# Attention's key blocks merged by predicated copies, PSUM banks redistributed and GpSimd jobs moved, in a fused attention and mixture-of-experts kernel

## The chip, the cores and the metric

The kernel runs on one core of a Trainium2 chip. The metric is the device time of one execution in microseconds, lower is better. The engines of a core run their own queues in order: TensorE (PE; PEld is its weight load), VectorE (DVE), ScalarE (ACT), GpSimd (POOL) and SyncE (SP), which here issues all transfers.

## The reference, cut to what matters

```python
# attention: q, k, v of (2, 8, 576, 64); window 128; ALiBi slopes per head
scores = (q @ k.T) / 8 + slope[h] * -abs(rel)      # rel = row - column
scores = where((rel >= 0) & (rel < 128), scores, -1e9)
attn = exp(scores - max); attn = attn / (attn.sum(-1) + 1e-9)
x = (attn @ v) as (1152, 512)
# first block: 4 experts with 1024 hidden columns each, all tokens through all of them
p = probs / (probs.sum(-1) + 1e-9)
x = sum over e of p[:, e] * (relu(x @ w1[e]) @ w2[e])
# second block: 2048 hidden columns
h = x @ w_in;  out = (h * cos(h)) @ w_out
```

All inputs and the output are fp32; w_in and w_out come in as double precision and are converted by the kernel.

## The kernel before, in words

**Attention.** The 576 rows of each of the two batch entries are cut into five units: unit 0 of 64 rows, units 1 to 4 of 128. A step is one unit and one half of the heads (g = 0 or 1, four heads each), 20 steps in all; unit numbers below are within a batch entry. The keys of a row lie in its own block and in the block ahead of it, so a unit from 1 on has scores of up to 256 columns, of which each row needs 128: where an own key would lie behind the row, the key at the same place of the block ahead is in the window. `attention` (from L464) emits at step k, in this order: `att_scores(k)`, `att_sums(k-1)`, `fill(k, 0)`, `att_transpose(k-3)`, `att_normalise(k-1)`, `fill(k, 1)`, `att_pv(k-4)`, `fill(k, 2)`. `att_scores` makes four score products into two PSUM tiles, then per head one VectorE pass (L362: adds bias and mask, keeps the minimum of the negated scores) and one ScalarE exponential with its sum (L367). `att_normalise` (L383) divides on GpSimd, `att_transpose` (L405) transposes each head's one or two blocks on TensorE and copies them out with VectorE (L415) and ScalarE (L417), `att_pv` (L433) multiplies with the values of both blocks. When both halves of a unit are done, its results leave PSUM: rounded into a high and a low part (`split_x`, L333), or through `transform` (from L273), a generator of nine parts (0 to 8) that builds seven combinations of the x tiles for a Strassen-like product, each as a high part on ScalarE (L278) and a low part, a subtraction (L130) on VectorE or GpSimd. `transformed` first issues what is left of the transform before, then part 0; `move(n)` issues n more parts. `fill` slips other work in: the weight jobs at steps 4 to 19, the first-layer products of group 0 that need plain x (`plain`) at steps 12 to 19 in halves, and the second-layer products `layer2(0, 0)`, `layer2(0, 1)`, `layer2(0, 2)` at steps 21, 22 and 23.

**The groups.** The two blocks are cut into 12 groups of 512 hidden columns: 0 to 7 are the experts, 8 to 11 the second block. Group 7 is called `turn` (its results are flipped by TensorE transposes, f1 to f8, and enter the second block through `transformed`). Every matrix is held as a high and a low part and each product is made of three passes (L537 for the combinations in `product`, L565 in `plain`, L631 in `layer2`). `pair` makes the combinations of two hidden tiles in seven products, in the order A11 B11, S2 T2, S1 T1, S3 T3, A12 B21, S4 B22, A22 T4: a step of `steps` (from L731) each, with ScalarE's copy p1 (L586), VectorE's additions u1 and c22 (L580) and `finish` between them. In groups 8 to 11 `finish` runs `cosine`, a chain of stages on ScalarE, VectorE and GpSimd (its last stage makes the low part of h or hpair, L517 and L130); `advance` issues one stage of every open chain. `layer2(g, t)` reads h for t under 3 and hpair above.

**What sets the order.** All of it is written out by hand, and each engine works through its queue in that order. `steps(g)` yields per TensorE step how many chain stages, weight jobs (`next(jobs)`) and conversion parts (`next(cv)`) are issued between its matmuls and its end; `run` (L783) issues matmuls, then `move(2)`, the stages, the jobs, the conversion parts, then the step's end. A weight job (L155, L172, L185, L130) rounds one 128x512 piece of a weight on ScalarE and subtracts on GpSimd, or makes two of the weight sums on GpSimd; some of them issue the next load on SP's queue. At the end of a group `run` issues what is left of the transforms:

```python
            while moved:
                move(24)
```

**PSUM.** Each bank takes one tile. `ps1` has two banks during the whole kernel; attention has three for scores, two for transposes, one for its results; after attention these six become `mm`. `bank()` (L674) numbers the product tiles: 4 are taken by `plain` and 3 by `layer2` during attention, and the first product of group 0 is number 8.

```python
    def bank():
        count[0] += 1
        return ps1 if mm is None or count[0] % 4 == 0 else mm
```

## Time and profile before

| what | value |
|---|---|
| median of 3 runs (lowest to highest) | 669.71 us (668.44 to 672.1) |
| the profiled execution | 668.45 us |
| its span | 666.7 us |
| busy: PE, PEld | 645.6 us (97%), 568.7 us (85%) |
| busy: DVE, ACT, POOL | 432.8, 335.9, 367.6 us |
| mean granted clock of TensorE | 0.995 |
| HBM | 90 GB/s over the span |

The span runs from the first to the last instruction; about 1.8 us of the execution's own time lie around it. Busy times say how long an engine had an instruction in work; matmuls are pipelined and their ends are modelled, so a busy TensorE is not TensorE at its peak, and gaps between its instructions are the surer sign.

### The profile page before, as it was taken

The page shows a single profiled execution, that of the slowest core. Times are in us where ns is not written, and L with a number is a line of the kernel's source. Part 1 is how long each engine was busy: PE and PEld are TensorE (multiplying, and loading weights), DVE is VectorE, ACT ScalarE, POOL GpSimd, SP SyncE. Part 2 cuts the span into 40 slices and gives each one's busy share as a digit, 9 for nine tenths or more (in the row PEclk, how much of TensorE's full clock was granted, in tenths as well). Part 3 has the DMA queues.
Part 4 walks back from the last instruction along what each step waited for, and adds up shares of the span by engine and source line. Part 5 has one row for each costly group of instructions (what it writes and reads, how often), then busy time and mean ns, then how long its engine had stood idle before and what let it go on. Part 6 is the DMA issues. An engine that isn't in the chain of part 4 may idle for free.

```text
span 666.7 us, 9755 instructions
## 1 busy us (share of the span) xinstructions
PE 645.6 (97%) x3516; PEld 568.7 (85%) x3516; DVE 432.8 (65%) x842; ACT 335.9 (50%) x768; POOL 367.6 (55%) x346
## 2 busy tenths in 40 slices
PE   8989899999999999999999999999799999999997
PEld 5677698998998998988988988988788988988976
DVE  7676776878668578589578562647663563563562
ACT  6878644453344354354343341346684674584560
POOL 3977729356265175183282381465468558558530
PEclk8999999999999999999999999999899999999999
DMA  9162114435417335245236130030101101202002
GB/s 262 41 204 83 32 33 138 130 112 200 128 35 225 106 101 185 79 139 193 80 131 200 32 121 7 32 96 0 33 0 64 65 0 63 65 0 64 17 31 94
DMA packets 39727, 60.40 MB, mean 91 GB/s; under 512 B 5632, under 2 KB 22016, under 8 KB 39680
## 3 DMA queue, kind: packets, MB, share of 16 engines
q1 hardware_dynamic: 39680, 59.80, 28.2%
q8 instruction: 27, 0.44, 0.3%
q14 instruction: 20, 0.16, 0.1%
HBM read 49.04 MB, written 10.75 MB: 90 GB/s over the span
## 4 chain that ended last, share of the span: by engine, by line
PE 78%; DVE 7%; ACT 7%; POOL 4%; issue 2%; DMA 1%; SPq 0%; ACTq 0%; DVEq 0%; POOLq 0%
PE o_ps L631 39%; PE o_ps L537 21%; PE o_ps L565 13%; PE s_ps L350 2%; DVE u L509 2%; ACT r L507 2%; ACT u L506 2%; PE x_ps L433 1%; POOL p L383 1%; POOL w1t L130 1%; PE t_ps L405 1%; POOL hpair L130 1%; DVE o_ps L580 1%; DVE xs L130 1%; DVE u L515 1%
## 5 line engine op out<-in xcount | busy, mean ns | idle before, releaser
L631 PE MATMUL o_ps<-w2t,hpair 128*128 128x512 f32 x864 | 207.3, 392 | 4.3 <-POOL hpair L130 4.1
L631 PEld LDWEIGHTS o_ps<-w2t,hpair 128*128 128x128 f32 x864 | 160.7, 188 | 38.3 <-POOL hpair L130 5.8
L537 PE MATMUL o_ps<-xs,w1t 128*128 128x384 f32 x1008 | 182.5, 338 | 3.9 <-DVE c L580 1.8
L537 PEld LDWEIGHTS o_ps<-xs,w1t 128*128 128x128 f32 x1008 | 177.1, 189 | 7.6 <-DVE c L580 3.1
L130 POOL TENSOR_TENSOR w2t<-raw,w2t 128x512 fp32r<-128x512 f32 x48 | 66.2, 1394 | 82.1 <-ACT w2t L185 82.1
L130 POOL TENSOR_TENSOR w1t<-raw,w1t 128x512 fp32r<-128x512 f32 x48 | 65.0, 1364 | 83.2 <-ACT w1t L155 83.0
L565 PE MATMUL o_ps<-xq,w1t 128*128 128x384 f32 x576 | 110.3, 338 | 0.0
L565 PEld LDWEIGHTS o_ps<-xq,w1t 128*128 128x128 f32 x576 | 101.6, 188 | 3.3
L631 PE MATMUL o_ps<-w2t,h 128*128 128x512 f32 x432 | 103.3, 392 | 0.0
L631 PEld LDWEIGHTS o_ps<-w2t,h 128*128 128x128 f32 x432 | 80.7, 188 | 16.1 <-issue 0.2
L130 POOL TENSOR_TENSOR w1t<-sm,w1t 128x512 fp32r<-128x512 f32 x48 | 64.6, 1356 | 41.9 <-ACT w1t L155 35.1
L509 DVE SCALAR_TENSOR_TENSOR u<-r,u 128x384 f32<-128x384 f32 x48 | 34.6, 726 | 51.7 <-ACT r L507 51.7
L130 POOL TENSOR_TENSOR hpair<-u,hpair 128x384 fp32r<-128x384 f32 x32 | 33.6, 1066 | 42.3 <-ACT hpair L517 42.3
L245 ACT ACTIVATE cr<-cr 128x512 f32<-128x512 f32 x32 | 21.6, 675 | 43.4 <-DVE cv L239 43.4
L367 ACT ACTIVATE p<-p,nmax 128x256 f32<-128x256 f32 (+2 forms) x80 | 36.2, 454 | 13.0 <-DVE nmax L362 12.8
L646 DVE SCALAR_TENSOR_TENSOR accpair<-o_ps,pr,accpair 128x512 f32<-128x512 f32 x42 | 31.3, 745 | 17.3 <-PE o_ps L631 17.3
L233 ACT ACTIVATE cr<-cr 128x512 int32<-128x512 uint32 x32 | 21.6, 675 | 40.7 <-DMA cr<-w_in 25.3
L524 ACT ACTIVATE hpair<-o_ps 128x384 fp32r<-128x384 f32 x48 | 23.4, 488 | 36.6 <-DVE o_ps L580 35.9
L155 ACT ACTIVATE w1t<-sm 128x512 fp32r<-128x512 f32 x48 | 30.0, 627 | 20.3 <-POOL sm L130 20.3
L525 DVE SCALAR_TENSOR_TENSOR hpair<-o_ps,hpair 128x384 fp32r<-128x384 f32 x48 | 26.6, 555 | 20.3 <-ACT hpair L524 20.3
L383 POOL TENSOR_TENSOR p<-p,rec 128x512 f32<-128x512 f32 (+5 forms) x30 | 32.6, 1102 | 9.5 <-DVE rec L377 5.6
L239 DVE SCALAR_TENSOR_TENSOR cv<-cr,cv 128x512 int32<-128x512 int32 x32 | 35.1, 1097 | 1.1
(100 smaller groups left out, 821.3 us busy)
## 6 DMA issues: line engine op xcount, KB each, us to landing
raw<-w SPq DMA_DIRECT2D x32, 512.0 KB, 3.7
cr<-w_in SPq DMA_DIRECT2D x16, 512.0 KB, 4.6
cr<-w_out SPq DMA_DIRECT2D x16, 512.0 KB, 4.5
wi<-cv SPq DMA_DIRECT2D x16, 256.0 KB, 3.6
wo<-cv SPq DMA_DIRECT2D x16, 256.0 KB, 2.3
raw<-wi SPq DMA_DIRECT2D x8, 512.0 KB, 3.5
raw<-wo SPq DMA_DIRECT2D x8, 512.0 KB, 3.5
qt<-qT SPq DMA_DIRECT2D x8, 256.0 KB, 4.9
```

The lines of the kernel that those rows point to most:

```text
L130: eng.tensor_tensor(out=out, in0=a, in1=b, op=ALU.subtract)
L155: nc.scalar.activation(out=hi[:, s], in_=src[:, s], func=AF.Copy)
L239: nc.vector.scalar_tensor_tensor(out=a, in0=hw, scalar=-0x40000000, in1=o, op0=ALU.bitwise_and, op1=ALU.bitwise_or,)
L367: nc.scalar.activation(out=p[:n, k, :wid], in_=p[:n, k, :wid], func=AF.Exp, scale=-1.0, bias=nmax[:n, k : k + 1], accum_out=den[:n, k, 0:1],)
L383: nc.gpsimd.tensor_tensor(out=p[:n, s, :wid], in0=p[:n, s, :wid], in1=rec[:n, s].unsqueeze(2).to_broadcast([n, s.stop - s.start, wid]), op ...
L509: nc.vector.scalar_tensor_tensor(out=u, in0=r, scalar=MAGIC, in1=u, op0=ALU.subtract, op1=ALU.subtract)
L524: nc.scalar.activation(out=hi, in_=src, func=AF.Relu)
L525: nc.vector.scalar_tensor_tensor(out=lo, in0=src, scalar=0.0, in1=hi.bitcast(F32), op0=ALU.max, op1=ALU.subtract)
L537: nc.tensor.matmul(ps, w(a, k, m), xs[:, bb, b, m], start=(start and m == 0 and (a, bb) == PASSES[0]), stop=(stop and m == 1 and (a, bb) = ...
L565: nc.tensor.matmul(ps, w(a, 2 * (q % 2) + d // 2, d % 2), xq[:, bb, d], start=(d == 0 and (a, bb) == PASSES[0]), stop=(d == ND - 1 and (a, ...
L631: nc.tensor.matmul(ps, h0[:, a, f, t * 128 : (t + 1) * 128] if t < NQ else hpair[:, a, f, (t - NQ) * 128 : (t - NQ + 1) * 128], w_t[2, g, ...
L646: nc.vector.scalar_tensor_tensor(out=o, in0=ps, scalar=s, in1=o, op0=ALU.mult, op1=ALU.add)
```

## The change

The scores of the block ahead are copied over those of the unit's own keys, where those lie behind the row: a mask `later` (nonzero there) steers two predicated copies on VectorE, within PSUM, and one block of 128 columns is left. Bias, exponential, normalising and transposing are done on it alone. With merged weights p, the product with the values is p times the values of the block ahead plus (p where the key is the unit's own, by the mask `own`) times the difference of the two blocks' values; the difference is made on GpSimd in `values`. Unit 1, whose block ahead has 64 rows, gets a tile `va` with those rows below 64 rows of zeros, loaded once more.

PSUM: `ps1` has one bank in place of two, scores four, transposes one, results two, and after attention `mm` has seven; `bank` takes ps1 for every eighth tile. Order: the weight jobs of groups 8 to 10 leave layer2(g, 1), layer2(g, 2) and P0 and go to layer2(g, 3), P1 and layer2(g, 4); the rest of a transform is not issued at the end of a group any more but carried on, one part behind each step of a pair. The diff, cut:

```diff
-    ps1 = pool("ps1", bufs=2, space=PSUM)
+    ps1 = pool("ps1", bufs=1, space=PSUM)
...
-    ptp = ap("ptp", bufs=4)
+    ptp = ap("ptp", bufs=2)
+    vdp = ap("vdp", bufs=3)
     stp = ap("stp", bufs=6)
-    ps_s = ap("ps_s", bufs=3, space=PSUM)
-    ps_t = ap("ps_t", bufs=2, space=PSUM)
-    ps_x = ap("ps_x", bufs=1, space=PSUM)
+    ps_s = ap("ps_s", bufs=4, space=PSUM)
+    ps_t = ap("ps_t", bufs=1, space=PSUM)
+    ps_x = ap("ps_x", bufs=2, space=PSUM)
...
+        for e in range(2):
+            for h in range(H):
+                slope = 2.0 ** (-8.0 * (h + 1) / H)
+                if e == 0:
+                    nc.vector.scalar_tensor_tensor(
+                        out=bm[:, e, h], in0=rel, scalar=-8.0 * slope, in1=edge,
+                        op0=ALU.mult, op1=ALU.add,
+                    )
+                else:
+                    nc.gpsimd.tensor_scalar(
+                        out=bm[:, e, h], in0=rel, scalar1=-8.0 * slope, scalar2=None, op0=ALU.mult
+                    )
+            if e == 0:
+                make_identity(nc, ident)
+        nc.gpsimd.memset(va[:64], 0.0)
+        nc.gpsimd.memset(own, 1.0)
...
+        if i == 1:
+            nc.sync.dma_start(out=va[64:], in_=v[b, :64, :])
+    def values(b, i):
+        ahead = va if i == 1 else v_t[b, i - 1]
+        vd = vdp.tile([128, DM], F32, name="vd", tag="vd")
+        nc.gpsimd.tensor_tensor(out=vd, in0=v_t[b, i], in1=ahead, op=ALU.subtract)
+        v_d[b, i] = ahead, vd
...
+        c0 = 128 - (s0 - k0)
...
                 nc.tensor.matmul(
-                    ps[hh][:n, m, :wid], q_t[u][r, 2 * g + m, :n],
+                    ps[hh][:n, m, c0 : 128 + n], q_t[u][r, 2 * g + m, :n],
                     k_t[b][r, 2 * g + m, k0 : s0 + n], start=True, stop=True,
                 )
-        p = ppool.tile([128, 4, 256], F32, name="p", tag="p")
+        p = ppool.tile([128, 4, 128], F32, name="p", tag="p")
...
+        if i:
+            for hh in range(2):
+                nc.vector.copy_predicated(
+                    ps[hh][:n, :, 128 + c0 :], later.bitcast(U32)[:n, :, c0:], ps[hh][:n, :, c0:128]
+                )
         for m in range(2):
             for hh in range(2):
                 k = 2 * m + hh
                 h = 4 * g + k
                 nc.vector.tensor_tensor_reduce(
-                    out=p[:n, k, :wid], in0=ps[hh][:n, m, :wid], in1=bm[:n, h, c0 : c0 + wid],
+                    out=p[:n, k, :n], in0=ps[hh][:n, m, 128 : 128 + n], in1=bm[:n, int(i > 1), h, :n],
                     scale=-0.125, scalar=3.0e38, op0=ALU.add, op1=ALU.min,
...
-        for s in (slice(0, 4),) if u[0] == 0 else (slice(0, 2), slice(2, 4)):
-            nc.gpsimd.tensor_tensor(
-                out=p[:n, s, :wid], in0=p[:n, s, :wid],
-                in1=rec[:n, s].unsqueeze(2).to_broadcast([n, s.stop - s.start, wid]), op=ALU.mult,
-            )
+        nc.gpsimd.tensor_tensor(
+            out=p[:n, :, :n], in0=p[:n, :, :n],
+            in1=rec[:n].unsqueeze(2).to_broadcast([n, 4, n]), op=ALU.mult,
+        )
         state[u, g] = p
...
+        if g == 0 and u[1]:
+            values(*u)
...
-        blocks = list(key_blocks(u[1]))
-        pT = []
-        for m in range(2):
-            tp = ps_t.tile([128, 2, 2, 128], F32, name="t_ps", tag="t_ps")
-            pt = ptp.tile([128, 2, 2, 128], F32, name="pt", tag="pt")
-            for bi, (j, o, ln) in enumerate(blocks):
-                for hh in range(2):
-                    nc.tensor.transpose(
-                        tp[:ln, bi, hh, :n], p[:n, 2 * m + hh, o : o + ln], ident[:n, :n]
-                    )
...
-            for a, bb in sl:
-                if m == 0:
-                    nc.vector.tensor_copy(pt[a, bb, :, :n], tp[a, bb, :, :n])
-                else:
-                    nc.scalar.activation(out=pt[a, bb, :, :n], in_=tp[a, bb, :, :n], func=AF.Copy)
-            pT.append(pt)
-        state[u, g] = pT
+        tp = ps_t.tile([128, 4, 128], F32, name="t_ps", tag="t_ps")
+        for k in range(4):
+            nc.tensor.transpose(tp[:n, k, :n], p[:n, k, :n], ident[:n, :n])
+        pt = ptp.tile([128, 4, 128], F32, name="pt", tag="pt")
+        nc.scalar.activation(out=pt[:n, :, :n], in_=tp[:n, :, :n], func=AF.Copy)
+        po = None
+        if u[1]:
+            po = ptp.tile([128, 4, 128], F32, name="po", tag="po")
+            nc.vector.tensor_tensor(
+                out=po, in0=tp, in1=own.unsqueeze(1).to_broadcast([128, 4, 128]), op=ALU.mult
+            )
+        state[u, g] = pt, po
 
...
-        pT = state.pop((u, g))
-        blocks = list(key_blocks(i))
...
         for m in range(2):
-            for bi, (j, o, ln) in enumerate(blocks):
-                for hh in range(2):
-                    h = 4 * g + 2 * m + hh
-                    nc.tensor.matmul(
-                        xt[64 * hh : 64 * hh + 64, 2 * g + m, :n],
-                        v_t[b, j][:ln, 64 * h : 64 * h + 64],
-                        pT[m][:ln, bi, hh, :n],
-                        start=(bi == 0), stop=(bi == len(blocks) - 1),
-                    )
+            for hh in range(2):
+                k = 2 * m + hh
+                h = 4 * g + k
+                hs = slice(64 * h, 64 * h + 64)
+                o = xt[64 * hh : 64 * hh + 64, 2 * g + m, :n]
+                if i == 0:
+                    nc.tensor.matmul(o, v_t[u][:n, hs], pt[:n, k, :n], start=True, stop=True)
+                    continue
+                ahead, more = v_d[u]
+                nc.tensor.matmul(o, ahead[:, hs], pt[:, k], start=True, stop=False)
+                nc.tensor.matmul(o, more[:, hs], po[:, k], start=False, stop=True)
...
-        return ps1 if mm is None or count[0] % 4 == 0 else mm
+        return ps1 if mm is None or count[0] % 8 == 0 else mm
...
-    mm = pool("mm", bufs=6, space=PSUM)
+    mm = pool("mm", bufs=7, space=PSUM)
...
-            yield layer2(g, 1), 2, 2 if turn else int(not last), 2
-            yield layer2(g, 2), 2, 2 if turn else int(not last), 2
+            yield layer2(g, 1), 2, 2 if turn else int(early), 2
+            yield layer2(g, 2), 2, 2 if turn else int(early), 2
...
-        njobs = 0 if last else 4 if turn else 6 if early else 10
+        njobs = [1] * 10
         if g == 0:
-            njobs += 2
+            njobs = [2, 2, 1, 1, 1, 1]
+        elif turn:
+            njobs = [1] * 4
+        elif early:
+            njobs = [1] * 6
+        elif not last:
+            njobs = [0, 1, 2, 2, 1, 2, 1, 1, 1, 1]
         for k, o in enumerate(order):
-            more = min(njobs, 2 if g == 0 and k < 2 else 1)
+            more = njobs.pop(0) if njobs and not last and str(o)[0] != "f" else 0
...
         for g in groups:
             for step, stages, njobs, ncv in steps(g):
                 next(step)
-                move(2)
+                move(2 if ncv or stages != 1 else 1)
                 for _ in range(stages):
                     advance()
                 for _ in range(njobs):
@@ -792,9 +821,6 @@
                 for _ in range(ncv):
                     next(cv, None)
                 next(step, None)
-            while moved:
-                move(24)
-
```

## Rows read from the trace of the kernel before

**Rows 1.** Busy by stage: us, each engine (instructions), granted clock, DMA share, GB/s.
```profile
13.00:39.00 26.00, 22.79 (x227) 15.75 (x226) 19.54 (x96) 23.09 (x84) 21.81 (x17) 1.00 0.41 118
39.00:70.50 31.50, 31.38 (x280) 24.42 (x280) 19.84 (x96) 24.65 (x87) 23.17 (x27) 1.00 0.34 108
...
88.20:422.00 333.80, 333.80 (x1687) 303.60 (x1686) 240.91 (x352) 132.94 (x252) 165.55 (x143) 1.00 0.37 119
...
499.90:667.00 167.10, 158.06 (x773) 139.21 (x772) 80.76 (x135) 88.31 (x181) 98.67 (x95) 1.00 0.14 46
```

**Rows 2.** Waits of PE over the span: total us, times, longest us.
```profile
PE o_ps L631 <- POOL hpair L130: 4.1, 4, 1.4
```

**Rows 3.** Timeline of PE, groups 7 to 8: start us, us, what.
```profile
473.88 1.32 PE L537 MATMUL o_ps<-xs,w1t 128*128 128x384 f32 x6 [1.69 <-ACT p L586]
476.50 3.91 PE L537 MATMUL o_ps<-xs,w1t 128*128 128x384 f32 x12 [1.31 <-DVE c L580]
```

**Rows 4.** Timeline of VectorE in attention: steps 6 and 19, then L644.
```profile
19.51 0.42 DVE L362 CUSTOM_DVE_ANT_0 p<-s_ps,bm 128x256 f32<-128x256 f32 x1
...
67.62 0.42 DVE L362 CUSTOM_DVE_ANT_0 p<-s_ps,bm 128x256 f32<-128x256 f32 x1 [1.84 <-PE s_ps L350]
...
91.25 0.75 DVE L644 TENSOR_SCALAR acc<-o_ps,pr 128x512 f32<-128x512 f32 x1
```

**Rows 5.** Timeline of PE, end of attention.
```profile
85.34 3.01 PE L631 MATMUL o_ps<-w2t,h 128*128 128x512 f32 x12
88.19 4.00 PE L537 MATMUL o_ps<-xs,w1t 128*128 128x384 f32 x22
```

**Rows 6.** The chain that ended last, attention: start us, us, what.
```profile
57.65 1.06 PE s_ps L350 x8
58.71 1.02 PE t_ps L405 x8
59.73 1.05 PE o_ps L565 x6
...
65.39 1.02 PE x_ps L433 x16
```

**Rows 7.** VectorE's groups by shape, 0:92: busy us, mean ns, idle before.
```profile
L362 DVE CUSTOM_DVE_ANT_0 p<-s_ps,bm 128x256 f32<-128x256 f32 x48 | 17.6, 421 | 5.9 <-PE s_ps L350 5.3 <-PE t_ps L405 0.2
L415 DVE COPY pt<-t_ps 128x512 f32<-128x512 f32 x12 | 8.0, 664 | 0.0
...
L362 DVE CUSTOM_DVE_ANT_0 p<-s_ps,bm 64x64 f32<-64x64 f32 x16 | 2.6, 211 | 0.9 <-PE s_ps L350 0.9
...
L130 DVE TENSOR_TENSOR xq<-x_ps,xq 128x512 fp32r<-128x512 f32 x2 | 1.4, 692 | 3.1 <-ACT xq L333 3.1
L130 DVE TENSOR_TENSOR tx<-x_ps,xk 128x256 f32<-128x256 f32 x3 | 1.3, 425 | 0.7 <-ACT xk L286 0.7
```

**Rows 8.** ScalarE's groups by shape, 0:92.
```profile
L367 ACT ACTIVATE p<-p,nmax 128x256 f32<-128x256 f32 x48 | 23.8, 498 | 6.5 <-DVE nmax L362 6.4
...
L417 ACT ACTIVATE pt<-t_ps 128x512 f32<-128x512 f32 x12 | 7.0, 579 | 0.9 <-PE t_ps L405 0.9
...
L367 ACT ACTIVATE p<-p,nmax 64x64 f32<-64x64 f32 x16 | 5.3, 335 | 4.8 <-DVE nmax L362 4.8
...
L155 ACT ACTIVATE w1t<-raw 128x512 fp32r<-128x512 f32 x4 | 2.5, 618 | 0.0
```

**Rows 9.** GpSimd's groups by shape, 0:92.
```profile
L130 POOL TENSOR_TENSOR w1t<-raw,w1t 128x512 fp32r<-128x512 f32 x4 | 5.1, 1269 | 3.5 <-ACT w1t L155 3.5
```

**Rows 10.** Timeline of ScalarE, step 11.
```profile
40.20 0.39 ACT L450 ACTIVATE xk<-x_ps 128x256 f32<-128x256 f32 x1 [1.14 <-DVE xq L130]
```

**Rows 11.** Busy times and granted clock (before the DMA share), groups 7 to 8.
```profile
478.00:479.00 1.00, 1.00 (x5) 1.00 (x5) 0.68 (x1) 0.91 (x3) 1.00 (x2) 0.50 0.00 0
```

**Rows 12.** Timeline of GpSimd, group 10.
```profile
598.09 1.28 POOL L130 TENSOR_TENSOR w1t<-raw,w1t 128x512 fp32r<-128x512 f32 x1
599.34 2.28 POOL L130 TENSOR_TENSOR hpair<-u,hpair 128x384 fp32r<-128x384 f32 x2
```

More of the change, by code (lines that the diff above doesn't have):

```diff
@@ L71, in tile_kernel @@
     ppool = ap("ppool", bufs=4)
-    ptp = ap("ptp", bufs=4)
+    ptp = ap("ptp", bufs=2)
+    vdp = ap("vdp", bufs=3)
     stp = ap("stp", bufs=6)
-    ps_s = ap("ps_s", bufs=3, space=PSUM)
-    ps_t = ap("ps_t", bufs=2, space=PSUM)
-    ps_x = ap("ps_x", bufs=1, space=PSUM)
+    ps_s = ap("ps_s", bufs=4, space=PSUM)
+    ps_t = ap("ps_t", bufs=1, space=PSUM)
+    ps_x = ap("ps_x", bufs=2, space=PSUM)
     ident = const.tile([128, 128], F32, name="ident")
-    scr = ppool.tile([128, 4, 256], F32, name="scr", tag="p")
@@ L81, in tile_kernel @@
-    bm = mkp.tile([128, H, 256], BF16, name="bm")
-    def constants():
-        rel_i, rel, msk = scr[:, 0].bitcast(I32), scr[:, 1], scr[:, 2]
-        nc.gpsimd.iota(rel_i, pattern=[[-1, 256]], base=WIN, channel_multiplier=1)
+    scr = ppool.tile([128, 4, 128], F32, name="scr", tag="p")
+    rel, edge = scr[:, 0], scr[:, 1]
+    later = mkp.tile([128, 2, 128], F32, name="later")
+    own = mkp.tile([128, 128], F32, name="own")
+    va = mkp.tile([128, DM], F32, name="va")
+    bm = mkp.tile([128, 2, H, 128], BF16, name="bm")
@@ L86, in constants @@
+    def constants():
+        rel_i = own.bitcast(I32)
+        nc.gpsimd.iota(rel_i, pattern=[[-1, 128]], base=0, channel_multiplier=1)
+        nc.gpsimd.memset(later, 0.0)
+        nc.gpsimd.affine_select(
+            out=later, in_=later, pattern=[[0, 2], [-1, 128]], compare_op=ALU.is_ge, fill=float(WIN),
+            base=0, channel_multiplier=1,
+        )
         nc.vector.tensor_copy(rel, rel_i)
-        nc.gpsimd.memset(msk, 0.0)
-        big = -8.0e9
+        nc.vector.tensor_tensor(out=rel, in0=rel, in1=later[:, 0], op=ALU.add)
+        nc.gpsimd.memset(edge, 0.0)
@@ L93, in constants @@
+        nc.gpsimd.memset(va[:64], 0.0)
+        nc.gpsimd.memset(own, 1.0)
         nc.gpsimd.affine_select(
-            out=msk, in_=msk, pattern=[[1, 256]], compare_op=ALU.is_ge, fill=big,
-            base=-1, channel_multiplier=-1,
-        )
-        for h in range(H):
-            slope = 2.0 ** (-8.0 * (h + 1) / H)
-            nc.vector.scalar_tensor_tensor(
-                out=bm[:, h, :], in0=rel, scalar=-8.0 * slope, in1=msk,
-                op0=ALU.mult, op1=ALU.add,
-            )
@@ L104, in constants @@
-        make_identity(nc, ident)
-    k_t, q_t, v_t = {}, {}, {}
+            out=own, in_=own, pattern=[[1, 128]], compare_op=ALU.is_ge, fill=0.0,
+            base=0, channel_multiplier=-1,
+        )
+    k_t, q_t, v_t, v_d = {}, {}, {}, {}
     def load_unit(b, i):
@@ L343, in att_scores @@
         k0 = UNITS[max(i - 1, 0)][0]
-        wid = s0 + n - k0
-        c0 = WIN if i == 0 else 256 - wid
+        c0 = 128 - (s0 - k0)
         ps = [ps_s.tile([128, 2, 256], F32, name="s_ps", tag="s_ps") for _ in range(2)]
@@ L367, in att_scores @@
                 nc.scalar.activation(
[L368 removed]
+                    out=p[:n, k, :n], in_=p[:n, k, :n], func=AF.Exp, scale=-1.0,
                     bias=nmax[:n, k : k + 1], accum_out=den[:n, k, 0:1],
                 )
[L371 removed]
+        state[u, g] = p, den, rec, n
     def att_sums(u, g):
@@ L682, in tile_kernel @@
     with tc.manual_schedule():
-        warm = ppool.tile([128, 4, 256], F32, name="warm", tag="p")
-        nc.vector.memset(warm[:, 0], 0.0)
+        warm = ppool.tile([128, 4, 128], F32, name="warm", tag="p").rearrange("p a b -> p (a b)")
+        nc.vector.memset(warm, 0.0)
         nc.vector.memset(dens, 1e-9)
@@ L689, in tile_kernel @@
                 ps1.tile([128, 512], F32, name="o_ps", tag="o_ps")[:, :256],
-                warm[:, 0, :128], warm[:, 0], start=True, stop=True,
+                warm[:, :128], warm[:, 256:], start=True, stop=True,
             )
@@ L773, in steps @@
                     yield half(halved, o[2] == "b"), 1, 0, 0
-            njobs -= more
     def half(step, end):
```

19 lines of the change are left out of this document (4 added, 15 removed).

## The prediction

> **What bounds the kernel now.** I read the busy times by stage first. In 88.2:422 PE is busy for all of its 333.8 us, in 39:70.5 for 31.38 of 31.5, in 13:39 only for 22.79 of 26, where ACT has more (23.09) [rows 1]. So TensorE's stream is the time, except in attention's early steps, where queues that wait for each other set it. Then the waits of PE: four for POOL's low parts of hpair, 4.1 us together [rows 2]. Then PE's timeline between groups 7 and 8, with gaps of 1.69 and 1.31 us [rows 3]. These the change can win; what it can lose is read from the end of attention [rows 4, 5] and from how its steps follow each other on VectorE [rows 4].
>
> **Attention, operations.** A step is one unit and one half of the heads; 16 of 20 have two key blocks.
> TensorE: 8 transposes take 1.02 us [rows 6], 4 half of that: 0.51 off in each of 16 steps, 8.2 us. Scores and the product with the values keep their counts.
> VectorE: a score pass takes 421 ns at 256 columns and 211 at 64 [rows 7], so about 281 at 128. Added are two predicated copies of 2 x 128 columns, PSUM to PSUM. No row shows one; the nearest is a subtraction of 256 columns out of PSUM, 425 ns [rows 7], the bounds are half of it (212) and two such passes (850). I take 425, so 0.85 per step. The multiplication by `own` takes the copy's place, 692 for 664 [rows 7].
> ScalarE: an exponential takes 498 ns at 256 columns and 335 at 64 [rows 8], so about 389 at 128: 0.44 off per step.
> GpSimd: half the columns to normalise, and a value difference (a 128x512 subtraction, 1269 [rows 9]) every second step; it is the fullest in neither stretch [rows 1]. The added load (the v rows of unit 0 once more) stands in SP's queue behind the unit's own three and is half of the last; scores need only the first two, so nothing; if the next unit's loads come late by it, half a landing. The constants: half the columns on VectorE, eight more operations on GpSimd, which has nothing else to do ahead of the first normalisation, so nothing; without that cover step 2 would start late by what is over.
>
> **Attention, the new chain.** ScalarE's copy and VectorE's multiplication now read one PSUM bank, the copy issued first. How such a pair behaves is seen at 40.20: ScalarE's copy out of x_ps sits idle for 1.14 us until VectorE's xq, issued before it, is through, though it uses nothing that xq makes: two readers of one bank go one after the other in the order of issue [rows 10]. Before, the two copies had a tile each. So at the end of each step VectorE's queue now stands until ScalarE has done four exponentials, the weight job and the copy, and behind the multiplication stand the next step's predicated copies and score passes, for which the next exponentials wait. One round: 2 x 0.425 + 0.281 to the first exponential, 4 x 0.389, a job 0.618, the copy 0.579 [rows 8], the multiplication 0.692: 4.6 us by durations; neighbours in one queue overlap by some 0.08 (three such joints) and more behind the passes, so 4.3. PE needs 1.06 for scores, 0.51, 1.05 for half a `plain` and 1.02 for values [rows 6], 3.6, and no longer sets the step.
> Steps 6 to 18 before: VectorE's first passes at 19.51 and 67.62 [rows 4], 48.1 us. After: eight full steps (6 to 9, 15 to 18) of 4.3, less 0.5 in steps 8 and 9 (no job on ScalarE), 0.5 more in 7, 9, 15 and 17 (a subtraction for x or `plain` follows): 35.4. Steps 10 to 14, with units 0 and 1 and `routing`, laid out in the same manner: 3.3, 4.6, 3.5, 3.4, 2.9: 17.7. Together 53.1, 5.0 more. Steps 2 to 5, where nothing is coupled yet, win 1.4 by shorter exponentials, laid out likewise. In steps 19 to 23 the transposes give about 0.4 back, the chain of the transform staying as it is, and one round of the coupling costs 0.3. So VectorE's tail ends y = 5.0 - 1.4 - 0.1 = 3.5 us later. Bounds of y: 8.2 earlier, if PE set every step; with copies of 850 ns 0.85 more in each of 13 steps, 14.5 later.
>
> **The bank at the head of group 0.** `count` is 7 when attention ends (4 `plain`, 3 `layer2`). The first product of group 0 is number 8, which by either rule goes to ps1. With two banks it reuses that of layer2(0, 1), read long before. With one it reuses that of layer2(0, 2), whose reader L644 is issued behind the whole last transform and ends at 91.25 + 0.75 = 92.0, while PE ends those matmuls at about 88.3 [rows 4, 5]. All of PE's queue stands behind that product. So group 0 begins at 92.0 + y in place of 88.3: 3.7 + 3.5 = 7.2 us later (bounds -4.5 and 18.2), and from there PE is full to 422, so nothing gives it back.
> [...]
> [...]
>
> **Groups 7 to 8.** Before, the first four products end at 472.2, then PE waits for ScalarE's copy of the first (queued behind the last roundings of the x tiles) and for VectorE's c22 [rows 3]. Now the end of that transform is spread, one part behind each step, and the copy comes earlier. I lay the queues out: products to 472.2, A12 by B21 to 473.2, S4 by B22 can start, but its second matmul reads GpSimd's low part of B22, now issued behind two weight jobs (steps 1 and 2 of the pair, 1.27 each by [rows 9]) and the low part of P2 (1.1, as hpair's [rows 12]); it takes half a job, 0.6. By ScalarE's queue P2's can start at about 471.3: 471.3 + 1.1 + 2.5 + 0.6 = 475.5. So 1.69 + 1.31 turn into one wait of about 2.1, and the other 11 matmuls (2.0 by [rows 5]) end at 477.6 against 476.50 + 3.91 = 480.4: 2.8 us won. [...] I take 2.8: single gaps of up to 1.4 us in 499.9:667 leave the clock at 1.00 [rows 1, 2], and 2.1 is nearer to them than to 3.0.
>
> **Jobs of groups 8 to 10.** Layer2(g, 6) waits for the third low part of hpair, which GpSimd starts late (599.34 is the third and fourth) because a weight job of 1.28 comes first [rows 12]. That job is moved behind layer2(g, 6). Three of the four waits are of this kind (the fourth is the last group's, which has no jobs, 0.7): 4.1 - 0.7 = 3.4, of which I leave 0.3 for the two parts ahead of the third: 3.1 won. The jobs land two each on steps 3, P1 and 4; nothing reads them before the next plain or pair, three steps on, and their loads have the same cover; without it a raw tile would be late by a landing. Early groups keep their places, and a bank still comes back after 8 tiles (1 + 7 for 2 + 6): nothing.
>
> **Sum.** 7.2 + 1.7 - 2.8 - 3.1 = +3.0. The profiled execution took 668.45 (span 666.7), 1.3 below the median of 669.71: 671.5 by the one, 672.7 by the other, and I forecast the median. 0.5% (3.3 us) is about what a measurement can tell from no change, so this lies just inside.
>
> **Rivals.**
> (a) Faster: VectorE isn't coupled to ScalarE, and the shorter work reaches the path. By the same laying out with uncoupled queues y is about -4.4, the bank costs -0.7 net, the sum is -4.9: 664.8. It decides from y = -2.9 on (sum under -3.4). For it: PE is nearly full in 39:70.5, where transposes go. Against: 40.20.
> (b) Groups 7 to 8 only change the name of their waits: GpSimd holds up B22 and the clock falls. Then 0 to -1.1 in place of -2.8, the sum +4.7 to +5.8: 675. For it: no single gap of 2.1 us is shown that keeps the clock.
> (c) The predicated copies are dear: they stand in front of the exponentials on the new chain, 0.2 us per step for 0.1 each, 2.6 us over 13 steps. At 850 the sum is +14: 684. For it: mask, source and target make three streams. Against: 256 columns out of PSUM take 421 and 425 ns in two forms [rows 7].
> (d) No wait at the head of group 0, because something releases the bank early: -3.7 - 1.7, the sum -2.4, 667.3. Against: L644 is last in VectorE's queue.
> (e) Another GpSimd piece takes the moved job's place: +3.1, the sum +6.1, 675.8. Against: none is queued there.
>
> **Chances.** Forecast 0.50, (a) 0.25, (b) 0.10, (c) 0.08, (d) 0.04, (e) 0.03. The forecast lies at the border: slower in 0.23, same in 0.27. (a) is faster in 0.22, else same; (b), (c) and (e) slower, (d) same. Faster 0.22, same 0.34, slower 0.44. Range: to 664.5, which keeps most of (a), and to 677.5, which leaves (c) out.
>
> **What would show it.** PE idle for some 4 us ahead of the first L537 of group 0, released by the VectorE operation behind layer2(0, 2); a granted clock near 0.5 behind it. VectorE's multiplication in attention released by ScalarE's copy, steps of 4.3 us and more; if they are near 3.6 and PE has no gaps, (a). One gap between groups 7 and 8 with a GpSimd `xs` as releaser. No POOL hpair waits in groups 8 to 10. The predicated copy near 425 ns; over 600, (c). Most likely to be wrong: y, since it adds up 13 steps.

## The result, and the profile after

The changed kernel takes 679.45 us in the median (677.0 to 680.78, four runs), the kernel before 669.69 beside it: ratio 1.0126, 95% interval 1.0095 to 1.0156. It is slower by 9.8 us, where the sum said 3.0 and the range ended at 677.5. The profiled execution has a span of 676.1 us, 9.4 more than before.

By stage (columns as in [rows 1]) PE is busy for 17.61 and 25.89 us where it was busy for 22.79 and 31.38, and its clock is 0.93 in the first stretch:

```profile
13.00:39.00 26.00, 17.61 (x176) 12.85 (x178) 16.07 (x89) 17.64 (x72) 19.63 (x19) 0.93 0.39 105
39.00:70.50 31.50, 25.89 (x239) 20.28 (x239) 19.32 (x107) 21.84 (x84) 20.97 (x21) 1.00 0.40 120
```

VectorE's operations by shape, and ScalarE's and GpSimd's new ones (0:98, as [rows 7 to 9]):

```profile
L399 DVE CUSTOM_DVE_ANT_0 p<-s_ps,bm 128x128 f32<-128x128 f32 x64 | 14.7, 285 | 0.0
L438 DVE TENSOR_TENSOR po<-t_ps,own 128x512 f32<-128x512 f32 x16 | 11.0, 688 | 21.3 <-ACT pt L434 21.3
L392 DVE COPY_PREDICATED s_ps<-later,s_ps 128x256 f32<-128x256 uint32 x24 | 9.0, 422 | 2.7 <-PE s_ps L382 2.7
...
L404 ACT ACTIVATE p<-p,nmax 128x128 f32<-128x128 f32 x64 | 24.9, 390 | 17.0 <-DVE nmax L399 16.9
L434 ACT ACTIVATE pt<-t_ps 128x512 f32<-128x512 f32 x16 | 9.2, 576 | 0.9 <-PE t_ps L432 0.9
...
L116 POOL TENSOR_SCALAR bm<-scr 128x128 bf16<-128x128 f32 x8 | 4.3, 556 | 0.3
```

The durations are those of the prediction: 285 for a pass (281), 422 for a predicated copy (425), 390 for an exponential (389). The coupling is there too: VectorE stands idle for 21.3 us ahead of its 16 multiplications, all for ScalarE's copy of the same bank. Its timeline at steps 6, 7 and 19 and at the end of attention (as [rows 4]):

```profile
19.40 0.69 DVE L438 TENSOR_TENSOR po<-t_ps,own 128x512 f32<-128x512 f32 x1 [1.80 <-ACT pt L434]
...
20.34 0.75 DVE L392 COPY_PREDICATED s_ps<-later,s_ps 128x256 f32<-128x256 uint32 x2
...
24.01 0.69 DVE L438 TENSOR_TENSOR po<-t_ps,own 128x512 f32<-128x512 f32 x1 [1.80 <-ACT pt L434]
...
73.09 0.75 DVE L392 COPY_PREDICATED s_ps<-later,s_ps 128x256 f32<-128x256 uint32 x2
...
97.21 0.74 DVE L668 TENSOR_SCALAR acc<-o_ps,pr 128x512 f32<-128x512 f32 x1
```

Steps 6 to 18 take 73.09 - 20.34 = 52.75 us (53.1 forecast, 48.11 before); but step 6 begins at 20.34, 0.83 later than before, where it should have been 1.4 earlier. PE at the head of group 0 (as [rows 5]) and its clock there (windows, columns as in [rows 11]):

```profile
90.79 3.02 PE L655 MATMUL o_ps<-w2t,h 128*128 128x512 f32 x12
98.10 2.26 PE L561 MATMUL o_ps<-xs,w1t 128*128 128x384 f32 x6 [4.28 <-DVE acc L668]
...
115.52 2.24 PE L589 MATMUL o_ps<-xq,w1t 128*128 128x384 f32 x12
```

```profile
94.00:96.00 2.00, 0.00 (x0) 0.00 (x0) 1.97 (x3) 0.80 (x3) 2.00 (x3) 1.00 0.04 16
96.00:98.00 2.00, 0.00 (x0) 0.00 (x0) 1.47 (x3) 0.42 (x1) 0.10 (x1) 0.83 0.00 0
98.00:100.00 2.00, 1.90 (x6) 1.93 (x7) 0.00 (x0) 0.00 (x0) 0.00 (x0) 0.50 0.00 0
...
104.00:105.00 1.00, 1.00 (x7) 1.00 (x7) 0.56 (x1) 0.00 (x0) 0.00 (x0) 0.94 0.00 0
```

The product waits for L668 as foretold. Behind the gap the clock is 0.50 for some 6 us, and the 84 products up to the first L589 take 17.42 us. Before they took 14.59, from 88.19 [rows 5] to here:

```profile
102.78 2.24 PE L565 MATMUL o_ps<-xq,w1t 128*128 128x384 f32 x12
```

Groups 7 to 8 (as [rows 3]), with the clock behind the second gap, and GpSimd there:

```profile
480.64 5.36 PE L561 MATMUL o_ps<-xs,w1t 128*128 128x384 f32 x29 [0.44 <-DVE xs L163]
486.40 0.41 PE L561 MATMUL o_ps<-xs,w1t 128*128 128x384 f32 x1 [0.41 <-DVE c L604]
488.62 2.89 PE L561 MATMUL o_ps<-xs,w1t 128*128 128x384 f32 x11 [1.81 <-POOL xs L163]
491.31 3.82 PE L655 MATMUL o_ps<-w2t,h 128*128 128x512 f32 x12
494.96 7.47 PE L561 MATMUL o_ps<-xs,w1t 128*128 128x384 f32 x42
```

```profile
490.00:491.00 1.00, 1.00 (x5) 1.00 (x5) 1.00 (x3) 0.22 (x1) 0.00 (x0) 0.50 0.43 150
```

```profile
484.99 2.71 POOL L163 TENSOR_TENSOR w2t<-raw,w2t 128x512 fp32r<-128x512 f32 x2
487.66 0.90 POOL L163 TENSOR_TENSOR xs<-accpair,xs 128x256 fp32r<-128x256 f32 x1
```

The two gaps of 1.69 and 1.31 have become 0.41 and 1.81, the second for the low part of B22 behind two weight jobs. From the pair's start (480.64) to 494.96 it is 14.32 us, before 15.12, between these two rows: 0.80 won.

```profile
467.90 4.28 PE L537 MATMUL o_ps<-xs,w1t 128*128 128x384 f32 x23 [0.44 <-DVE xs L130]
...
483.02 7.47 PE L537 MATMUL o_ps<-xs,w1t 128*128 128x384 f32 x42
```

Of the hpair waits [rows 2] two are left:

```profile
PE o_ps L655 <- POOL hpair L163: 0.8, 2, 0.7
```

### The profile page after: what moved, and what is told of

Read it like the earlier page. It is cut to its first block, busy times and chain, and to the rows that moved or that the text cites. A ratio compares the mean times of both kernels' runs of the same rounds, so it can differ in the third digit from the quotient of the medians.

```text
span 676.1 us, 9665 instructions
## 1 busy us (share of the span) xinstructions
PE 641.7 (95%) x3452; PEld 566.2 (84%) x3452; DVE 435.5 (64%) x867; ACT 329.8 (49%) x764; POOL 368.9 (55%) x356
## 4 chain that ended last, share of the span: by engine, by line
PE 74%; DVE 10%; ACT 8%; POOL 3%; issue 3%; DMA 1%; SPq 0%; DVEq 0%; ACTq 0%; POOLq 0%
PE o_ps L655 37%; PE o_ps L561 21%; PE o_ps L589 13%; ACT p L404 2%; DVE u L533 2%; ACT r L531 1%; ACT u L530 1%; POOL hpair L163 1%; PE s_ps L382 1%; DVE po L438 1%; DVE xs L163 1%; DVE u L539 1%; ACT pt L434 1%; DVE o_ps L604 1%; DVE tx L163 1%
## 5 line engine op out<-in xcount | busy, mean ns | idle before, releaser
L561 PE MATMUL o_ps<-xs,w1t 128*128 128x384 f32 x1008 | 185.0, 340 | 8.0 <-DVE acc L668 4.3
L589 PE MATMUL o_ps<-xq,w1t 128*128 128x384 f32 x576 | 110.4, 338 | 0.0
L589 PEld LDWEIGHTS o_ps<-xq,w1t 128*128 128x128 f32 x576 | 101.6, 188 | 3.3
L533 DVE SCALAR_TENSOR_TENSOR u<-r,u 128x384 f32<-128x384 f32 x48 | 38.9, 817 | 60.9 <-ACT r L531 59.5
L404 ACT ACTIVATE p<-p,nmax 128x128 f32<-128x128 f32 (+1 forms) x80 | 30.2, 379 | 24.3 <-DVE nmax L399 24.2
L272 DVE SCALAR_TENSOR_TENSOR cv<-cr,cv 128x512 int32<-128x512 int32 x32 | 33.7, 1053 | 1.1
L537 ACT ACTIVATE u<-u 128x384 f32<-128x384 f32 x48 | 24.7, 518 | 18.4 <-DVE u L533 18.3
```

What stands on the lines that cost most here:

```text
L272: nc.vector.scalar_tensor_tensor(out=a, in0=hw, scalar=-0x40000000, in1=o, op0=ALU.bitwise_and, op1=ALU.bitwise_or,)
L404: nc.scalar.activation(out=p[:n, k, :n], in_=p[:n, k, :n], func=AF.Exp, scale=-1.0, bias=nmax[:n, k : k + 1], accum_out=den[:n, k, 0:1],)
L533: nc.vector.scalar_tensor_tensor(out=u, in0=r, scalar=MAGIC, in1=u, op0=ALU.subtract, op1=ALU.subtract)
L537: nc.scalar.activation(out=u, in_=u, func=AF.Sin, scale=-TWOPI)
L561: nc.tensor.matmul(ps, w(a, k, m), xs[:, bb, b, m], start=(start and m == 0 and (a, bb) == PASSES[0]), stop=(stop and m == 1 and (a, bb) = ...
L589: nc.tensor.matmul(ps, w(a, 2 * (q % 2) + d // 2, d % 2), xq[:, bb, d], start=(d == 0 and (a, bb) == PASSES[0]), stop=(d == ND - 1 and (a, ...
```

## The experiments

Each set of four ran beside the kernel before (medians 670.54, 670.33 and 671.07 us); ratios are to that, with their 95% intervals.

**Another tile to the single bank.**

```diff
-        return ps1 if mm is None or count[0] % 8 == 0 else mm
+        return ps1 if mm is None or count[0] % 8 == 7 else mm
```

> Changed kernel, but of every 8 result tiles the one with remainder 7 goes to the single bank, so the first product of group 0 (tile 8) gets a free bank. My theory (the wait stands only in front of that one tile, and the half clock behind it is the wait's doing): PE's 4.28 us of idle time ahead of group 0 is gone, group 0 starts near 93.9 in place of 98.10, the first 84 products take 14.4 in place of 17.4, together 7.3 us less: about 672.2. Rival 1 (the wait only moves to the next tile that needs VectorE, which is as late): a wait of 3 us and more on another tile in 94:104, time within 2 us of 679.5. Rival 2 (the clock falls for attention's own gaps, not for this one): clock still 0.50 behind 98, gain 4.3 only, about 675.2.

Measured: 672.99 us, ratio 1.0023 (0.9999 to 1.0047). PE around the head of group 0:

```profile
92.86 3.02 PE L655 MATMUL o_ps<-w2t,h 128*128 128x512 f32 x12
95.71 5.50 PE L561 MATMUL o_ps<-xs,w1t 128*128 128x384 f32 x30
```

No gap is left, and the 84 products take 15.03 us (95.71 to 110.74), 2.39 less than 17.42. Gap and clock together are 6.7 us of the loss, near the 6.5 by which the medians differ (6.9 by the two ratios). Both rivals are out: the wait went to no other tile, and the slow clock behind 98 was that gap's. In this profile attention itself ended 2.07 us later, though its instructions are the same (last section).

**VectorE's multiplication first.**

```diff
         pt = ptp.tile([128, 4, 128], F32, name="pt", tag="pt")
-        nc.scalar.activation(out=pt[:n, :, :n], in_=tp[:n, :, :n], func=AF.Copy)
         po = None
...
+        nc.scalar.activation(out=pt[:n, :, :n], in_=tp[:n, :, :n], func=AF.Copy)
         state[u, g] = pt, po
```

> Changed kernel with VectorE's multiplication by own issued before ScalarE's copy of the same bank. Theory (VectorE is held up because its read was issued behind ScalarE's, which stands behind four exponentials and a weight job): the VectorE waits of 1.80 and 1.27 us on pt are gone, full steps take 3.6 to 3.9 in place of 4.3 to 4.8, steps 6 to 18 together 46 to 49 in place of 52.75, VectorE's tail 4 to 7 us earlier, and the time 673 to 676. Rival (one transposition bank: PE's transposes wait until the last reader is through, and that is still ScalarE's copy behind its queue): steps stay at 4.2 and more with PE's wait on pt grown, time within 1.5 us of 679.5.

Measured: 675.97 us, ratio 1.0076 (1.0047 to 1.0104). VectorE at steps 6, 16 and 19, and after the last scores:

```profile
20.01 0.75 DVE L392 COPY_PREDICATED s_ps<-later,s_ps 128x256 f32<-128x256 uint32 x2
...
57.43 0.66 DVE L437 TENSOR_TENSOR po<-t_ps,own 128x512 f32<-128x512 f32 x1
...
67.42 0.76 DVE L392 COPY_PREDICATED s_ps<-later,s_ps 128x256 f32<-128x256 uint32 x2 [1.18 <-PE s_ps L382]
...
74.64 0.66 DVE L437 TENSOR_TENSOR po<-t_ps,own 128x512 f32<-128x512 f32 x1
```

The waits for pt are gone and steps 6 to 18 take 47.41 us, 5.34 less: the order of the two readers was the coupling. VectorE's last operation of attention ends only 2.8 us earlier (95.14), because behind step 19 the same order works the other way: VectorE has the transform to do, and ScalarE's copy stands for it (2.10 us idle ahead of the one at 75.39). From step 19 to the end the tail takes 27.72 us, for 24.86 in the changed kernel. The tail's 4 to 7 us did not come.

**The warm-up in four banks, and with it the bias tiles on VectorE.**

```diff
-                ps1.tile([128, 512], F32, name="o_ps", tag="o_ps")[:, :256],
+                ps_s.tile([128, 2, 256], F32, name="s_ps", tag="s_ps")[:, 0],
...
-                    nc.gpsimd.tensor_scalar(
+                    nc.vector.tensor_scalar(
                         out=bm[:, e, h], in0=rel, scalar1=-8.0 * slope, scalar2=None, op0=ALU.mult
```

The first of these has only the warm-up's lines:

> Changed kernel with the four warm-up products of the start in four banks of the scores instead of one single bank. Theory (the start is late because these products now follow each other through one bank: 1.27 us each, 5.06 in all for 3.78 before): they end near 5.3, first scores near 5.3 in place of 6.50, VectorE's step 6 between 19.1 and 19.7 in place of 20.34, time 0.6 to 1.3 less, about 678.5. Rival (GpSimd's constants, which end at 8.50, set when step 0 can be normalised): scores earlier, but the first normalisation at 8.5 or later, step 6 not before 19.9, time within 0.4 of 679.5.

> As the kernel before it in this set, and the eight bias tiles that the change gave GpSimd (4.5 us there) are made by VectorE. If GpSimd's constants hold up the first normalisation once the scores are early: normalisation near 7.9, step 6 another 0.5 to 1.0 earlier than in that kernel, time another 0.5 to 1.0 less. If they do not: VectorE's 2 us more of constants stand ahead of its first passes, step 0 starts no earlier than in the changed kernel, and the gain of the warm-up is lost.

Measured: 678.41 us, ratio 1.0115 (1.0079 to 1.0151), and 678.58, ratio 1.0108 (1.0071 to 1.0145): no gain that can be told apart. The warm-up of the changed kernel, then PE with the warm-up's edit alone, and its clock:

```profile
1.51 5.06 PE L712 MATMUL o_ps<-warm 128*128 128x256 f32 x8 [1.51 <-DVE dens L710]
```

```profile
1.51 3.78 PE L712 MATMUL s_ps<-warm 128*128 128x256 f32 x8 [1.51 <-DVE dens L710]
5.22 1.12 PE L382 MATMUL s_ps<-xk,qt 64*64 64x64 f32 x16
...
13.98 2.08 PE L382 MATMUL s_ps<-xk,qt 64*128 64x256 f32 x8
```

```profile
14.00:16.00 2.00, 2.00 (x11) 1.18 (x9) 0.00 (x0) 1.41 (x6) 1.19 (x2) 0.50 1.21 273
```

The first scores come 1.28 us earlier, yet step 6 is at 20.70, later than 20.34. One reason was in the expectation (the first normalisation starts at 8.48, where GpSimd's constants end); the other was not: PE now waits sooner (1.47 us at 13.22 for 1.32 at 13.87), and the scores of step 5 run at a clock of 0.50, 2.08 us for 1.13. With the bias tiles on VectorE step 6 is at 19.86, and the clock is 0.50 from 12 to 24.

**Spare products to keep PE busy**, on top of those two edits:

```diff
+            if s == 1 and 0 < k < 7:
+                spare = ps1.tile([128, 512], F32, name="o_ps", tag="o_ps")
+                for _ in range(4):
+                    nc.tensor.matmul(spare[:, :128], ident, ident, start=True, stop=True)
```

> The kernel with the early warm-up and the bias tiles on VectorE, and in steps 1 to 6 four products of the unit matrix by itself into the spare single bank, which nothing reads (0.2 us each, 5 us in all), so that PE idles less. Theory (step 6 is no earlier there because the clock falls to 0.50 between 11 and 25): clock 1.00 through 8:25, step 6 of VectorE at 18.0 to 19.0 in place of 19.86, steps 6 and 7 of 4.3 and 4.9, group 0 1 to 2 us earlier than in that kernel (98.92). Rival (queues set step 6): clock 1.00 but step 6 at 19.5 or later.

Measured: 677.94 us, ratio 1.0111 (1.0082 to 1.014). The clock stays at 1.00 from 4 to 38 us, but step 6 is at 21.28: each set of four takes 1.06 to 1.78 us of PE's queue, 7.4 in all, where the author's estimate, from no row, was 0.8, so the spare products take the place that the clock gives back. The theory's size is refuted. The rival's row (clock 1.00, step 6 later than 19.5) is met, but these products alone can make it, so how much an early start with a clock of 1.00 would bring stays open.

**Two banks for the transposed probabilities again.**

```diff
-    ps_t = ap("ps_t", bufs=1, space=PSUM)
-    ps_x = ap("ps_x", bufs=2, space=PSUM)
+    ps_t = ap("ps_t", bufs=2, space=PSUM)
+    ps_x = ap("ps_x", bufs=1, space=PSUM)
```

> Changed kernel with two banks for the transposed probabilities and one for attention's results, as before the change. Theory (the two readers of one bank go one after the other, and that alone couples the queues; the number of such banks does not matter): VectorE still waits 1.27 to 1.80 us for ScalarE's pt in each full step, steps 6 to 18 take 52 to 54 together, time within 2 us of 679.5. Rival (PE's transposes wait for the one bank and make the step): steps 6 to 18 in 49 or less, time 3 us or more lower.

Measured: 677.81 us, ratio 1.0115 (1.0075 to 1.0155). The waits of 1.80 us are all there, and steps 6 to 18 take 73.75 - 21.40 = 52.35. The number of banks is not what makes the step. PE's transposes of step 1 now start at 12.16 (13.87 in the changed kernel), but PE then stands for 1.48 us ahead of the values of step 0, for ScalarE's copy of that step, and the scores of step 5 come no earlier: 14.67 for 14.55. Step 6 is 1.06 later than in the changed kernel; the scores of step 5 took 2.08 us for 1.13, at a clock of 0.52 (14:16).

**The weight jobs of group 8 behind the low part of B22.**

```diff
-                    more = g > 0 and 1 <= k <= 2
+                    more = g > 0 and (4 <= k <= 5 if g == NG1 else 1 <= k <= 2)
```

> Changed kernel, but in group 8 the two weight jobs of the first pair stand behind its fifth and sixth product in place of its second and third, so behind GpSimd's low part of B22 in GpSimd's queue. Theory (what ate the gain between groups 7 and 8 is that low part queued behind two weight jobs of 2.7 us, and the half clock behind the gap): PE's wait of 1.81 us on GpSimd's xs at 488.62 is gone or under 0.5, the granted clock stays above 0.9 in the 8 us behind it, and the next group of products starts 3.0 to 3.6 us earlier against the pair's start: about 676.2. Rival 1 (ScalarE and VectorE are behind too, the gap is only renamed): a wait of 1.3 us or more on another operand, gain under 1. Rival 2 (the weight jobs are then late for layer 2): a wait of layer2(8, 0) on w2t, gain under 1.

Measured: 678.53 us, ratio 1.0105 (1.0067 to 1.0143). PE:

```profile
489.75 2.52 PE L561 MATMUL o_ps<-xs,w1t 128*128 128x384 f32 x12 [0.39 <-ACT h L541]
492.11 2.47 PE L655 MATMUL o_ps<-w2t,h 128*128 128x512 f32 x10
495.25 0.73 PE L655 MATMUL o_ps<-w2t,h 128*128 128x512 f32 x2 [0.68 <-POOL w2t L163]
495.82 7.92 PE L561 MATMUL o_ps<-xs,w1t 128*128 128x384 f32 x42
```

The gap of 1.81 is gone, the clock is 1.00 from 480 to 498, and the stretch from the pair's start (483.98) to the next products is 11.84 us for 14.32: 2.48 won, less than the 3.0 because the weights are now 0.68 late for layer 2, as the second rival has it in part. The time does not show it (about 676.2 was expected): in this profile group 0 began at 101.59 in place of 98.10, for the same attention.

**The kernel before with one single bank.**

```diff
-    ps1 = pool("ps1", bufs=2, space=PSUM)
+    ps1 = pool("ps1", bufs=1, space=PSUM)
...
-        return ps1 if mm is None or count[0] % 4 == 0 else mm
+        return ps1 if mm is None or count[0] % 8 == 0 else mm
...
-    mm = pool("mm", bufs=6, space=PSUM)
+    mm = pool("mm", bufs=7, space=PSUM)
```

> Kernel before with one single bank in place of two and seven in place of six behind attention, every eighth tile to the single one; attention as before. Theory: the first product of group 0 waits for VectorE's last operation of attention (near 92.0), a gap of about 3.7 us ahead of it, and the half clock behind the gap costs up to 3.0: group 0 ends 5 to 7 us later than before, plus what the warm-up products through one bank cost at the start (up to 1.3 us later scores; 0 to 1.3 in time): about 676. Rival (the clock fell in the changed kernel because attention there was full of gaps, not because of this one): a gap of 3.7 with the clock at 1.00 behind it, about 673.5.

Measured: 677.39 us, ratio 1.0102 (1.0072 to 1.0133).

```profile
95.48 16.35 PE L537 MATMUL o_ps<-xs,w1t 128*128 128x384 f32 x84 [3.75 <-DVE acc L644]
```

The gap is 3.75 us (3.7 by the prediction's rows), and the 84 products take 16.19 us (to 111.67) for 14.59: the fall of the clock (0.50 at 96:98, 0.80 at 98:100) costs 1.6 here. Attention ends 3.4 later, where 0 to 1.3 was expected. Of that 1.28 is the warm-up, which takes 5.06 us as in the changed kernel. The rest is not separated: in 12:20 PE is busy for all 8.00 us with 45 instructions, before for 7.07 us with 63, and in the next profile, where attention has no edit and also ends 1.4 later than before's, for 8.00 us with 52. This part of the change alone makes the old kernel about as slow as the whole change does.

**The kernel before with the new order of jobs in groups 8 to 10.**

```diff
-        njobs = 0 if last else 4 if turn else 6 if early else 10
+        elif not last:
+            njobs = [0, 1, 2, 2, 1, 2, 1, 1, 1, 1]
```

> Kernel before with only the order of the weight jobs in groups 8 to 10 changed, as the change has it. Theory: three of PE's four waits for GpSimd's low parts of hpair are gone, 4.1 us of them fall to 0.8 or less, time 2.5 to 3.1 lower than before, about 667. Rival (the GpSimd pieces set loose land on other stages: in the changed kernel the pairs of these groups took 0.55 longer each): gain under 1.5.

Measured: 668.75 us, ratio 0.9968 (0.9946 to 0.999). The waits for hpair fall to 0.8, and the three layer-2 groups behind them are 0.97, 1.22 and 1.24 us shorter; but the three pairs that follow are 0.48, 0.60 and 0.62 longer, as this one, 578.96 to 589.38 where it was 579.56 to 589.38:

```profile
578.96 7.89 PE L537 MATMUL o_ps<-xs,w1t 128*128 128x384 f32 x42
587.19 2.35 PE L537 MATMUL o_ps<-xs,w1t 128*128 128x384 f32 x12 [0.34 <-DVE c L580]
```

Net 1.7 us: half of what is won is given back in the next stage. PE's waits there are put down to ScalarE's copy p and VectorE's c; which piece delays these was not separated. Between groups 7 and 8, which this edit leaves alone, the same gaps of 1.69 and 1.31 us left the clock at 1.00 in this profile, and the 12 products behind them took 2.37 us for the 3.91 of [rows 3]. Of the 1.54 so won, 1.20 were lost again in the next pair, where PE waits 0.69 for ScalarE's copy. So behind the same two gaps the clock was 0.50 in one profile and 1.00 in the other, and of the 1.54 us between them 0.34 were left one pair later.

**The edits together.** The changed kernel with the bank, the jobs of group 8, and VectorE first up to step 19:

```diff
+        first = 2 * units.index(u) + g > 16
+        if first:
+            copy()
         po = None
...
+        if not first:
+            copy()
```

> Changed kernel with three edits: another tile than number 8 to the single bank; VectorE's multiplication issued ahead of ScalarE's copy up to step 19 and behind it from step 20 on, where VectorE has the transform to do; in group 8 the two weight jobs behind GpSimd's low part of B22. Theory (these three places made the loss): step 19 of VectorE near 67.4, its tail near 92.3, group 0 starts within 1.5 us of before's 88.35 with no gap and no half clock, groups 7 to 8 are 3.3 and the late groups 2.3 us shorter than before: about 664.5. Rival (attention's gaps make the clock fall early and eat the steps' gain): group 0 starts 2 us and more later than before, 667 or more.

> As the kernel before it in this set, with the warm-up products in the banks of the scores and the eight bias tiles on VectorE. If the start sets the rest: another 0.7 to 1.5 less. If an earlier start only leaves PE idle sooner, so that the clock falls in the first 25 us (as in the two kernels that had these edits alone): no gain, or up to 1 us more.

Measured: 666.66 us, ratio 0.993 (0.9907 to 0.9954), and with the early start 665.5, ratio 0.9923 (0.9895 to 0.9951). Both beat both kernels, by less than was expected of the first, 664.5: step 19 was at 68.70 in place of 67.4, its clock fell to 0.50 from 18 to 22 and again at 78:80, and group 0 began at 90.85, 2.7 later than before's 88.19, as the rival has it. In the second the clock is 0.50 from 14 to 18 and 1.00 from 20 on, and the tail from step 19 takes 24.90 us, so issuing ScalarE's copy first there does what it was meant to. Group 0 began here:

```profile
88.51 9.80 PE L566 MATMUL o_ps<-xs,w1t 128*128 128x384 f32 x53
```

The 1.2 us between the two medians lie within their intervals, so what the early start is worth is not shown.

**Only what the change does behind attention**, on the kernel before: the new lists, one part of the transform behind each step, no drain at the end of a group, and group 8's two jobs late.

```diff
-                move(2)
+                move(2 if ncv or stages != 1 else 1)
...
-            while moved:
-                move(24)
```

> Kernel before with attention and its banks untouched, and everything that the change does behind attention: no drain of the transform at the end of a group, its parts one behind each step, the new order of weight jobs in groups 8 to 10, and the two weight jobs of group 8 behind the low part of B22. Theory: groups 7 to 8 win 3.3, the late groups 1.7 to 2.3: about 665. Rival (this gain needs the seven banks that the change gives these stages): under 3 us won, 667.5 or more.

Measured: 664.53 us, ratio 0.9915 (0.9889 to 0.9941), the lowest median of all, though not to be told from 665.5. Groups 7 to 8 take 11.83 us (467.93 to 479.76) for 15.12, and the rest behind them is 1.64 shorter. The rival is out: the gain does not need the seven banks. So of the versions with the losses mended that were found, the one with the old attention is as fast (its group 0 begins at 88.23, for 88.51): no gain of the new attention can be told.

## Why the prediction was wrong

The sum was +3.0; the profiled execution is 9.4 longer. Term by term, forecast and measured:

| term | forecast | measured |
|---|---|---|
| VectorE's tail: steps 2 to 5 | -1.4 | +0.83 |
| steps 6 to 18 | +5.0 | +4.64 |
| steps 19 to 23 | -0.1 | +0.48 |
| bank at the head of group 0, beyond the tail | +3.7 | +3.96 |
| fall of the clock there | +1.7 | +2.83 |
| groups 7 to 8 | -2.8 | -0.80 |
| jobs of groups 8 to 10 | -3.1 | -2.25 |
| end of the kernel | 0 | -0.3 |

These mechanisms were right, each at its place: two readers of one bank went in the order of issue and tied VectorE to ScalarE (21.3 us of waits; VectorE's multiplication issued first takes steps 6 to 18 from 52.75 to 47.41 us, two banks leave them at 52.35); the single bank holds up group 0 (two experiments, from either side: 4.28 us gone, 3.75 come); GpSimd's order makes the hpair waits (4.1 us, 0.8 with the new order); groups 7 to 8 keep one wait of 1.81 us for B22. What failed are four terms, all to the same side: a late start that the sum did not have, a clock that was to hold and fell, and the sizes of the other fall and of the jobs.

The largest is the step "Steps 2 to 5, where nothing is coupled yet, win 1.4 by shorter exponentials". It put the start of the kernel at nothing, and left out another user of the single bank, the warm-up. Its four products go through one bank, 5.06 us for 3.78, and they begin 0.33 later, since VectorE now fills an operand of 512 columns in place of 256 (0.48 us for 0.27). So PE's first scores come at 6.50 in place of 4.90. What becomes of that is read on ScalarE, from its first exponential to its copy `xq`, which step 6 of VectorE stands behind; before, then after:

```profile
5.88 0.35 ACT L367 ACTIVATE p<-p,nmax 64x64 f32<-64x64 f32 x1 [3.87 <-DVE nmax L362]
...
18.77 0.37 ACT L333 ACTIVATE xq<-x_ps 128x256 fp32r<-128x256 f32 x1
```

```profile
7.48 0.35 ACT L404 ACTIVATE p<-p,nmax 64x64 f32<-64x64 f32 x1 [5.41 <-DVE nmax L399]
...
19.27 0.36 ACT L366 ACTIVATE xq<-x_ps 128x256 fp32r<-128x256 f32 x1
```

ScalarE begins 1.60 us later and needs 11.79 us in place of 12.89, so its shorter work did win 1.10 of the 1.4. "Nothing is coupled yet" is not right either: the multiplication at 19.40, which waits 1.80 us for ScalarE, stands ahead of step 6, and with VectorE first step 6 comes at 20.01, 0.33 earlier. 1.60 - 1.10 + 0.33 is the measured 0.83.

On the way PE waits too: ScalarE's copy of step 0 starts at 13.36 (before at 12.28), and PE's transposes of step 1 wait 1.32 at 13.87, with the scores of step 5 behind them (the row names GpSimd's p, but that was through at 11.82; ScalarE's copy ended at 13.72). Two banks for the transposes only move that wait to the values of step 0, so it is ScalarE's lateness and not this bank. The sum is that of one pair of profiles: mending the warm-up alone did not bring step 6 forward, since the clock then fell.

The second is in groups 7 to 8, "2.1 is nearer to them than to 3.0", by which the clock was to hold (3.0 are before's two gaps, with a clock of 0.50 behind them [rows 3, 11]; 475.5 + 2.0 there is 477.5, not 477.6, which changes nothing). The gaps were 0.41 and 1.81, 2.2 together, and the clock fell to 0.50 behind them: this is rival (b), "0 to -1.1 in place of -2.8", and the 0.80 won lies just under its 1.1. With the gap taken away by the moved jobs the stretch won 3.28 against before.

The sum's 1.7 for a fall of the clock is the difference between the 3.91 us of 12 products at 0.50 [rows 3, 11] and the 2.2 that 22 in 4.00 us [rows 5] give for as many, an estimate; no run shows it as the price of a fall at the head of group 0. There the old kernel with one bank lost 1.6 and the changed one 2.83 against before, 2.39 against the same kernel without the gap, whose products take 0.44 more than before's at a clock of 1.00 [rows 1].

The jobs' 3.1 stood for the layer-2 groups alone, where 3.4 was measured; the 0.5 and 0.6 that pairs lose behind them were not looked for. Rival (e) named another piece in that same stage; the loss was in the next one.

Of the other rivals, (c) is out with 422 ns a copy, (d) with the wait of 4.28 us, and (a) is answered by the experiment that uncouples the queues: the steps take 47.4 us, but VectorE's tail ends at 95.14, 3.1 later than before where (a) had 4.4 earlier, and the time is still 675.97.

The sum has no term for the clock within attention. Before's was 1.00 in 13:39, with PE idle for 12% of it [rows 1], but just ahead of that stretch it is down (columns as there):

```profile
8.00:12.00 4.00, 3.31 (x20) 2.23 (x18) 3.14 (x21) 3.99 (x19) 1.14 (x3) 0.65 1.06 355
```

The changed kernel leaves PE idle for 32% of 13:39, its clock is 0.93 there, and with another tile on the single bank, on the same attention, it is 0.50 from 14 to 26 us. So the clock went between 0.50 and 1.00 within attention, in profiles of the same instructions too, and the prediction lacked a term for it. What sets it there is not shown; with two banks for the transposes it is 0.52 at 14:16 as well.

## What to carry to other kernels

When a pool of PSUM banks is cut to one, list all its users in order, the warm-up and the first tile of the next stage included, and for each the last reader and what stands ahead of that reader in its queue. Where two engines read one bank, issue that one first whose queue is shorter at that place, which can differ between a loop and its tail (VectorE first: 47.41 us for 52.75 in steps 6 to 18, 27.72 for 24.86 from step 19 on). A gain from moved jobs is counted through the stage where they land, and a gap in front of a full TensorE with the clock of 0.50 that can follow it (here the 84 products took 1.6 us more behind a gap of 3.75 us and 2.83 more behind 4.28).
